# One core, attention plus a gated feed-forward block: engines in written order, row-tiled score tails, row-major sums, Silu on ACT, K transposed by DMA and O by one DMA per step

## The chip, the cores and the metric

The kernel runs on one core of a Trainium2 chip. The metric is the device time of that core in microseconds (us); each kernel was run several times and the median is quoted. The engines are called as the profile calls them: PE (matrix engine), PEld (its weight loads), DVE (vector engine), ACT (scalar engine), POOL (GpSimd), SP (the engine that issues most DMAs).

## The reference, cut to what matters

```python
xn = layernorm(x)                                  # x: 2048 x 640, bf16
q  = (xn @ wq)                                     # 32 heads of 192
k, v = last 512 of the 2048 rows of each head's cache
p  = softmax(q @ k.T * 192**-0.5)                  # no mask
s  = concat_heads(p @ v) @ wo                      # wo: 6144 x 640
g  = silu((silu(xn @ w_gate) * (xn @ w_up)) @ w_down)   # F = 1536
return x + s * g
```

The kernels take two heads at a time ("a pair"; 16 pairs) and 512 rows of x at a time ("a block"; 4 blocks). They subtract the mean over the keys from K, which a softmax does not notice. A head has 192 = 128 + 64 columns: a "main" part that fills the 128 rows of the PE array, and a "tail" of 64.

## The kernel before

Its instructions are placed by a scheduler. Four parts matter. First, K is transposed by PE, main parts as 128x128 tiles and tails as column tiles of the array (128x64). Second, the tails of the two heads of a pair share one 128-row tile of Q, and the K tail of a head is padded with zeros in the other head's rows, so that a tail costs as much as a main:

```python
for kc in range(KC):                       # K transposes
    nc.tensor.transpose(kt[:, 0, kc*P:(kc+1)*P], K_cur[:, hh, kc, 0:DM], ident[:])
for kc in range(KC):
    nc.tensor.transpose(kt[tb:tb+DT, 1, kc*P:(kc+1)*P], K_cur[:, hh, kc, DM:Dh], ident[:])
nc.vector.memset(khat[ob_rows, 1, :], 0.0)
...
for kc in range(KC):                       # scores: one tile of 512 columns, two buffers
    sc = aps.tile([P, 512], dt.float32, name="sc", tag="sc", bufs=2)
    nc.tensor.matmul(sc[:], khat[:, 0, kc*P:(kc+1)*P], qT_m[:, cols], start=True, stop=False)
    nc.tensor.matmul(sc[:], khat[:, 1, kc*P:(kc+1)*P], qT_tail[:, cols], start=False, stop=True)
    p_t = ppool.tile([P, 512], dt.bfloat16, name="p_t")
    nc.scalar.activation(p_t[:], sc[:], ACT.Exp, scale=att_scale)
```

Third, the output projection is computed transposed (512 rows of x as columns) and summed over the pairs in `saccT`, so that the end needs transposes of fp32 tiles. Fourth, O is transposed by 240 small DMAs.

```python
for j in range(3):                         # output projection, transposed
    nc.tensor.matmul(sT_ps[:, :], wo_t[:, j, c*P:(c+1)*P], OT_t[:, j, b*512:(b+1)*512], ...)
nc.vector.tensor_tensor(saccT[:, c, cols], saccT[:, c, cols], sT_ps[:, :], ALU.add)
...
for c in range(c0 // P, c1 // P):          # final tile: fp32 transposes back
    nc.tensor.transpose(so_ps[:, cc*P:(cc+1)*P], saccT[:, c, t*P:(t+1)*P], identf[:])
nc.vector.tensor_tensor(prod[:, c0:c1], so_ps[:, 0:c1-c0], g2_t[:, c0:c1], ALU.mult)
...
nc.gpsimd.tensor_tensor(ob[:], prod[:], x_t[:], ALU.add)
```

The softmax here doesn't subtract the row's maximum and nothing guards it: scores larger than these inputs give would overflow.

## Time and profile before

The median is 1082.95 us (1082.24 to 1084.11). Split into three stretches, of which the last begins with the start of the last exp, the kernel spends:

| stretch | before, us | PE busy in it |
|---|---|---|
| launch to first score matmul (layernorm, feed-forward) | 205.7 | 182.5 |
| first score matmul to start of the last exp (attention) | 848.0 | 842.1 |
| start of the last exp to the end (drain) | 29.4 | 16.4 |

The table is read from the windows view of before; each line has the window, its length, then the busy time of PE, PEld, DVE, ACT and POOL (with the number of instructions), the granted PE clock (1.00 is full), the share of the DMA engines and GB/s:

```profile
0.00:205.70 205.70, 182.45 (x1020) 90.09 (x1020) 103.26 (x195) 61.51 (x98) 27.72 (x47) 0.99 0.24 83
205.70:1053.70 848.00, 842.13 (x5195) 468.08 (x5196) 551.62 (x1830) 400.79 (x709) 107.95 (x150) 1.00 0.25 60
1053.70:1083.10 29.40, 16.36 (x109) 9.86 (x106) 16.70 (x41) 2.35 (x4) 20.14 (x24) 0.86 0.43 139
```

PE is the bound. The page of before says so in the busy line (busy us, share of the span, instructions) and in the chain of waits:

```profile
PE 1040.9 (96%) x6320; PEld 568.0 (52%) x6320; DVE 671.6 (62%) x2065; ACT 464.7 (43%) x811; POOL 155.8 (14%) x219
PE 91%; DMA 2%; DVE 2%; POOL 1%; ACT 1%; issue 1%; POOLq 0%; SPq 0%; ACTq 0%; DVEq 0%
```

Busy is not the same as streaming. The trace's matmul durations are modelled: 379 ns for a 512-column matmul although the next one starts 215 to 216 ns later. What counts is the distance between starts: 216 ns for 512 columns, 83 for 193, 56 for 128, in both kernels, and 136 for 320, which only the changed one has. Summing these (and 109 for an fp32 transpose) over all matmuls gives 992 us of streaming before. The groups that the change touches are these (line, engine, operation, out<-in, shapes, count; then busy us and mean ns; then idle time before it and its releaser):

```profile
L392 ACT ACTIVATE p_t<-sc 128x512 bf16<-128x512 f32 x512 | 286.3, 595 | 318.7 <-PE sc L387 318.5
L263 PE MATMUL sT_ps<-OT_p,wo_p 128*128 128x512 bf16 x960 | 257.4, 379 | 1.1 <-DVE saccT L274 0.6
L274 DVE TENSOR_TENSOR saccT<-saccT,sT_ps 128x512 f32<-128x512 f32 x300 | 202.0, 680 | 44.0 <-PE sT_ps L263 41.0
L404 PE MATMUL pv<-V_h,p_t 128*128 128x193 bf16 x2048 | 213.7, 246 | 0.0
L387 PE MATMUL sc<-qT_tail,khat 128*128 128x512 bf16 x512 | 191.0, 379 | 1.2 <-DVE khat L375 1.2
L362 PE MATMUL kt<-ident,K_p 128*128 128x128 bf16 x128 | 14.8, 219 | 0.1
L364 PE MATMUL kt<-ident,K_p 128*64 128x128 bf16 x128 | 13.1, 225 | 0.0
```

L387 is the zero-padded tail: 512 matmuls of 216 ns, 110 us of streaming, half of it zeros. L362 and L364 are the K transposes.

The timeline of before shows small losses that neither busy time nor the waits view records (start us, us, engine, line, operation, out<-in, count):

```profile
311.28 0.41 PE L404 MATMUL pv<-V_h,p_t 128*128 128x193 bf16 x3
311.70 0.38 PE L383 MATMUL sc<-qT_m_2929,khat 128*128 128x512 bf16 x1
311.91 0.38 PE L387 MATMUL sc<-qT_tail,khat 128*128 128x512 bf16 x1
312.18 0.38 PE L383 MATMUL sc<-qT_m_2929,khat 128*128 128x512 bf16 x1
```

Three PV matmuls need 0.25 us, but the score matmul after them starts 0.42 us later. From 311.91 to 312.18 it is 0.27 instead of 0.216: the next score tile is still being read by an exp. The modelled durations (0.41, 0.38) cover these gaps, so the view of waits shows next to nothing.

The timeline also shows what a change of the array's tiling costs:

```profile
302.03 0.39 PE L362 MATMUL kt<-ident,K_p 128*128 128x128 bf16 x4
302.34 0.41 PE L364 MATMUL kt<-ident,K_p 128*64 128x128 bf16 x4
302.69 0.82 PE L263 MATMUL sT_ps<-OT_p,wo_p 128*128 128x512 bf16 x3
```

Four 56 ns transposes take 0.22 us, but the column-tiled ones start 0.31 us after the first: the last hand-over is 149 ns, 93 more than 56. On the way out it is 151 to 152.

### The profile page before, as it was taken

To read this page: it belongs to the slowest core of one execution; us is meant where nothing else is said; L and a number is where in the kernel's file an instruction comes from. 1 tells how busy PE (TensorE), PEld (TensorE's weight loads), DVE (VectorE), ACT (ScalarE), POOL (GpSimd) and SP (SyncE) were. 2 spreads that over 40 slices of the span, in tenths; PEclk is the share of its full clock that TensorE was granted. 3 is DMA by queue.
4 is the path that set the end of the run, shared out by engine and by line. 5 is a ranking of instruction groups with operands and counts; after the bars stand their busy time and mean duration, and the time that the engine had idled before them with its cause. 6 is when DMAs were issued, how large, how long until landed. Compare 5 with 4: busy or idle time off the path is not lost.

```text
span 1083.1 us, 17198 instructions
## 1 busy us (share of the span) xinstructions
PE 1040.9 (96%) x6320; PEld 568.0 (52%) x6320; DVE 671.6 (62%) x2065; ACT 464.7 (43%) x811; POOL 155.8 (14%) x219
## 2 busy tenths in 40 slices
PE   2999999899999999999999999999999999999985
PEld 1454444465555555555555555555555555555553
DVE  6644544263566757575758484848484848575775
ACT  2422222456545454535354545354544444444520
POOL 4400000200111111111111111111102010000066
PEclk9999999999999999999999999999999999999998
DMA  9400000212323131313131313131313140302034
GB/s 353 123 25 13 13 25 19 88 44 50 88 52 78 48 81 45 81 44 83 43 85 42 86 44 84 42 81 44 87 39 93 33 84 22 86 8 59 1 108 136
DMA packets 118724, 72.05 MB, mean 67 GB/s; under 512 B 103536, under 2 KB 110192, under 8 KB 118640
## 3 DMA queue, kind: packets, MB, share of 16 engines
q0 software_dynamic: 12080, 39.47, 12.5%
q1 hardware_dynamic: 106560, 31.49, 12.2%
q8 instruction: 50, 0.82, 0.3%
q14 instruction: 34, 0.28, 0.1%
HBM read 42.07 MB, written 5.24 MB: 44 GB/s over the span
## 4 chain that ended last, share of the span: by engine, by line
PE 91%; DMA 2%; DVE 2%; POOL 1%; ACT 1%; issue 1%; POOLq 0%; SPq 0%; ACTq 0%; DVEq 0%
PE sT_ps L263 19%; PE pv L404 15%; PE sc L383 12%; PE sc L387 10%; PE qkA L332 6%; PE qkB L339 6%; PE qkC L346 6%; PE gu L200 5%; PE gu L205 5%; PE dn L222 2%; DMA x_blk<-in_A_x_dram 2%; ACT p_t L392 1%; PE kt L364 1%; POOL ob L300 1%; PE kt L362 1%
## 5 line engine op out<-in xcount | busy, mean ns | idle before, releaser
L392 ACT ACTIVATE p_t<-sc 128x512 bf16<-128x512 f32 x512 | 286.3, 595 | 318.7 <-PE sc L387 318.5
L263 PE MATMUL sT_ps<-OT_p,wo_p 128*128 128x512 bf16 x960 | 257.4, 379 | 1.1 <-DVE saccT L274 0.6
L274 DVE TENSOR_TENSOR saccT<-saccT,sT_ps 128x512 f32<-128x512 f32 x300 | 202.0, 680 | 44.0 <-PE sT_ps L263 41.0
L404 PE MATMUL pv<-V_h,p_t 128*128 128x193 bf16 x2048 | 213.7, 246 | 0.0
L404 PEld LDWEIGHTS <-p_t 128*128 128x128 bf16 x2048 | 176.7, 97 | 60.7 <-DVE O_p L421 13.5
L387 PE MATMUL sc<-qT_tail,khat 128*128 128x512 bf16 x512 | 191.0, 379 | 1.2 <-DVE khat L375 1.2
L372 DVE TENSOR_REDUCE ssum<-kt 128x1 f32<-128x512 bf16 x64 | 43.7, 684 | 160.4 <-PE kt L364 160.1
L263 PEld LDWEIGHTS <-wo_p 128*128 128x128 bf16 x960 | 89.8, 97 | 92.7 <-issue 2.5
L412 DVE RECIPROCAL r<-pv 128x1 f32<-128x1 f32 x512 | 74.4, 159 | 75.5 <-PE pv L404 75.5
L414 DVE TENSOR_SCALAR O_p<-pv,r 128x192 bf16<-128x192 f32 x256 | 102.3, 414 | 7.0 <-DVE r L412 3.7
L124 POOL DMA_DIRECT2D V_h<-in_A_v_cache_dram x32 | 24.7, 772 | 461.7 <-PE sc L387 266.6
L421 DVE TENSOR_SCALAR O_p<-pv,r 128x128 bf16<-128x128 f32 x256 | 87.6, 342 | 0.0
L332 PE MATMUL qkA<-xnT,wq_p 128*128 128x512 bf16 x320 | 85.5, 383 | 1.6 <-DVE g_t L229 1.6
L387 PEld LDWEIGHTS <-khat 128*128 128x128 bf16 x512 | 49.3, 97 | 68.3 <-issue 39.2
L339 PE MATMUL qkB<-xnT,wq_p 128*128 128x512 bf16 x320 | 84.6, 380 | 0.0
L346 PE MATMUL qkC<-xnT,wq_p 128*128 128x512 bf16 x320 | 80.1, 379 | 0.0
L418 DVE TENSOR_SCALAR O_p<-pv,r 128x64 bf16<-128x64 f32 x256 | 72.1, 282 | 5.2
L383 PEld LDWEIGHTS <-khat 128*128 128x128 bf16 x512 | 49.3, 97 | 46.1 <-DVE khat L375 4.5
L200 PE MATMUL gu<-xnT,wg_sb 128*128 128x512 bf16 x240 | 60.2, 380 | 0.8 <-DVE hT L213 0.8
L210 ACT ACTIVATE sig<-gu 128x512 bf16<-128x512 f32 x48 | 28.7, 597 | 75.2 <-PE gu L205 75.2
L205 PE MATMUL gu<-xnT,wu_sb 128*128 128x512 bf16 x240 | 60.3, 382 | 0.0
L343 ACT CAST qT_tail<-qkB 128x512 bf16<-128x512 f32 x63 | 36.9, 585 | 50.7 <-PE qkB L339 50.7
(168 smaller groups left out, 931.0 us busy)
## 6 DMA issues: line engine op xcount, KB each, us to landing
K_p<-in_A_k_cache_dram POOLq DMA_DIRECT2D x16, 384.0 KB, 3.5
V_h<-in_A_v_cache_dram POOLq DMA_DIRECT2D x32, 192.0 KB, 3.2
wo_p<-in_A_wo_dram POOLq DMA_DIRECT2D x32, 160.0 KB, 2.6
wq_p<-in_A_wq_dram POOLq DMA_DIRECT2D x16, 240.0 KB, 3.8
OT_p<-O_p SPq DMA_TRANSPOSE x240, 2.3
x_blk<-in_A_x_dram SPq DMA_DIRECT2D x4, 640.0 KB, 9.5
wq_p<-in_A_wq_dram POOLq DMA_DIRECT2D x16, 160.0 KB, 3.2
wo_p<-in_A_wo_dram POOLq DMA_DIRECT2D x32, 80.0 KB, 2.5
```

The costliest lines, as they stand in the source:

```text
L200: nc.tensor.matmul(gu[:, 0, :], wg_sb[:, c, f * P : (f + 1) * P], xnT[:, c, qcols], start=(c == 0), stop=(c == NC - 1),)
L205: nc.tensor.matmul(gu[:, 1, :], wu_sb[:, c, f * P : (f + 1) * P], xnT[:, c, qcols], start=(c == 0), stop=(c == NC - 1),)
L263: nc.tensor.matmul(sT_ps[:, :], wo_t[:, j, c * P : (c + 1) * P], OT_t[:, j, b * 512 : (b + 1) * 512], start=(j == 0), stop=(j == 2),)
L274: nc.vector.tensor_tensor(saccT[:, c, b * 512 : (b + 1) * 512], saccT[:, c, b * 512 : (b + 1) * 512], sT_ps[:, :], ALU.add,)
L332: nc.tensor.matmul(qkA[:, :], wq_cur[:, c, 0:DM], xnT[:, c, cols], start=(c == 0), stop=(c == NC - 1),)
L339: nc.tensor.matmul(qkB[:, :], wq_cur[:, c, DM : DM + 2 * DT], xnT[:, c, cols], start=(c == 0), stop=(c == NC - 1),)
L346: nc.tensor.matmul(qkC[:, :], wq_cur[:, c, Dh + DT : 2 * Dh], xnT[:, c, cols], start=(c == 0), stop=(c == NC - 1),)
L383: nc.tensor.matmul(sc[:], khat[:, 0, kc * P : (kc + 1) * P], qT_m[:, b * 512 : (b + 1) * 512], start=True, stop=False,)
L387: nc.tensor.matmul(sc[:], khat[:, 1, kc * P : (kc + 1) * P], qT_tail[:, b * 512 : (b + 1) * 512], start=False, stop=True,)
L392: nc.scalar.activation(p_t[:], sc[:], ACT.Exp, scale=att_scale)
L404: nc.tensor.matmul(pv[:, s, 0 : Dh + 1], Ps[kc][:, qt * P : (qt + 1) * P], V_h[:, kc, 0 : Dh + 1], start=(kc == 0), stop=(kc == KC - 1),)
L414: nc.vector.tensor_scalar(O_p[:, t, 0:Dh], pv[:, s, 0:Dh], r[:], None, op0=ALU.mult)
```

## The change

It is a rewrite with one intent: keep PE streaming, and stream fewer columns. Every engine is given its instructions in the order in which they are written. A step is one block of one pair (64 steps), and PE's stream in a step mixes work of four steps: scores of step i, PV of step i-1, output projection of step i-3, Q of step i+1. The core of the diff, cuts marked by "...":

```diff
+    ctx.enter_context(tc.manual_schedule())
...
-                    nc.tensor.transpose(kt[:, 0, kc * P : (kc + 1) * P], K_cur[:, hh, kc, 0:DM], ident[:])
+        nc.sync.dma_start_transpose(
+            out=d["KT"][:, 0:3, j * P : (j + 1) * P],
+            in_=d["K"][:, j, :, :].rearrange("p h d -> p (h d)"),
+        )
...
+    def scores(i, kcs):                       # two key chunks, two heads: two tiles of 2 x 512
+        scs = [(kc, sc_tile()) for kc in kcs]
+        for kc, sc in scs:
+            for h in range(2):
+                nc.tensor.matmul(sc[:, h, :], khat[:, 2 * h, ks], qT[:, 2 * h, :], start=True, stop=False)
+        for kc, sc in scs:
+            for h in range(2):
+                r = slice(h * 64, (h + 1) * 64)       # tails: 64 rows, no padding
+                nc.tensor.matmul(sc[:, h, :], khat[r, 1, ks], qT[r, 1, :], start=False, stop=True)
+        for kc, sc in scs:
+            nc.scalar.activation(p_t[:, :, :], sc[:, :, :], ACT.Exp, scale=scale)
...
+    def wo_half(i, qt, n):                    # output projection, row-major, 320 columns
+        ps = mm_tile()                        # mm: two buffers, shared with Q
+        for j in range(3):
+            nc.tensor.matmul(ps[:, 0:HD], OTs[i][:, 3 * qt + j, :], pairs[pr]["wo"][:, j, cols], ...)
+        ...
+            nc.vector.tensor_tensor(sacc[:, t, cols], sacc[:, t, cols], ps[:, 0:HD], ALU.add)
+            if pr == NPAIR - 2 and n == 1:
+                pre_final(t)                  # GpSimd: load x, sacc = sacc * g + x
+        else:                                 # last pair
+            if i >= NS - 2 and n == 0:
+                nc.scalar.copy(s_f[:], ps[:, 0:HD])
+                nc.gpsimd.tensor_tensor(s_f[:], s_f[:], g2[:, t, cols], ALU.mult)
+                nc.gpsimd.tensor_tensor(obs[t][:, cols], s_f[:], sacc[:, t, cols], ALU.add)
+            else:
+                nc.vector.tensor_tensor(s_f[:], ps[:, 0:HD], g2[:, t, cols], ALU.mult)
+                nc.vector.tensor_tensor(obs[t][:, cols], s_f[:], sacc[:, t, cols], ALU.add)
...
+            order = ("A", 0, 1, "q0", 2, 3, "B", 4, "q1", 5, 6, "q2", 7)
+        for step in order:      # "A", "B": two key chunks of scores; "q0".."q2": Q;
+            ...                 # a number: a "unit", one wo_half and then one PV of 4 matmuls
```

Also: Silu comes from ACT's own function instead of Sigmoid and a multiply; g stays on chip; a step's O is transposed by one DMA (63 in all) instead of four; 16 warm-up matmuls and small x loads precede the weights.

## The prediction

> **What bounds the kernel now.** TensorE. The busy table gives PE 1040.9 of 1083.1 us, DVE 671.6, ACT 464.7; the chain of waits is 91% PE. The PE clock is near full speed throughout. Successive matmul starts in the timeline: 216 ns for 512 columns, 83 to 86 ns for 193 (PV), about 56 ns for 128. So streamed columns bound PE, with three losses: (a) the start: x is first used at 23.7 us, gate matmuls run steadily only from 34.7; (b) PV-to-score hand-overs that take about 250 ns instead of 85, and score-to-score ones of 273 instead of 216, because two one-bank score tiles wait for a 595 ns exp: about 25 us; (c) the hand-over to attention (204 to 211 us) and the final stage (1026 to 1083 us, PE 41 of 57 us), about 20 us together.
>
> **What the change removes, adds, moves (PE).**
> - K transposes (256) go to DMA: their line sums give -23 us, with their mode switches.
> - fp32 output transposes go (sums are row-major): -14 us.
> - Score tails: 512 zero-padded 512-column matmuls become 512 matmuls of 64 rows, in pairs on different row halves. The Trainium skill (TensorE: Matmul & The Clock Gate, Part 3) says such matmuls run concurrently; no run shows it yet. If so -55 us (256 x 216 ns).
> - Against that, the skill (TensorEngine Tiling, Key Properties) says a change of tiling mode drains the array. The trace agrees for column tiles: 128x128 to 128x64 and back costs 149 to 152 ns instead of 56, so 95 ns a switch. 256 switches: +24 us.
> - Output projection: 960 x 216 becomes 1536 x about 136 (estimate, 320 columns): neutral.
>
> **Other engines, per step of 64** (estimates from the traced durations): ACT 4 exps of 1024 columns at about 1.02 us plus 3 casts of 0.585 = 5.8 us; DVE 8 sums at 0.48, 4 normalisations at 0.55, reciprocals, K: about 7.4 us. PE: 15x216 + 8x216 + 4x216 + 32x85 + 24x136 = 11.8 us, plus 0.38 us of switches. PE stays the bound; score tiles now own four banks with filler between, so loss (b) should mostly vanish. The two projection buffers may wait on DVE/ACT: I allow 0.2 us a step.
>
> **Sum.** First gate matmul at 11 us (small x pieces ahead of weights); FFN 163 us of streaming plus 4; attention 64 x 12.4 = 793 us; drain after PE's work about 8 us (GpSimd arithmetic, store). Total about **980 us** (0.905 of before); 8 in 10: 952 to 1022. Faster by over 2%: 0.95; within: 0.03; slower: 0.02.
>
> **What would show each step.** Groups: tail matmuls L355 starting in pairs within a few ns, four tails in about 0.43 to 0.6 us. Timeline: a step repeats every 12.2 to 12.5 us. Waits: PE waits for exp nearly nil; waits of L412 for DVE and L158 for ACT under 0.3 us a step. First gate matmul near 11 us. DMA table: O transposes (4x larger) land in well under a 12 us step; no L412 weight load waits for them. DVE 55 to 60% busy, ACT about 40%.
>
> **What would make it wrong.** Tails serial: +55 us (about 1035). Switches dearer for row halves than the 95 ns measured for column halves: each 100 ns is 26 us. Projection buffers stalling PE: each 0.5 us a step is 32 us. O transposes by DMA slower than a step: one stall per step.

## The result, and the profile after

The changed kernel takes 1005.28 us (1004.59 to 1007.32), against 1082.97 us for the one before in the same rounds. The ratio is 0.9282, with a 95% interval of 0.9268 to 0.9295. A ratio here is always the mean time of one kernel's runs over the mean of the other's runs of the same rounds, so it is not quite the ratio of the medians. The prediction was 980 with a range of 952 to 1022: the time lies in the range, 25 us above the centre. All outputs are right.

Here are the busy line of the page after, the groups that answer to those above, and the three stretches in the windows view of after:

```profile
PE 974.6 (97%) x6540; PEld 564.7 (56%) x6540; DVE 522.7 (52%) x1265; ACT 421.1 (42%) x561; POOL 151.5 (15%) x188
L419 DVE TENSOR_TENSOR sacc<-sacc,mm 128x320 f32<-128x320 f32 x448 | 217.6, 486 | 294.4 <-PE mm L412 291.7
L360 ACT ACTIVATE p_t<-sc 128x1024 bf16<-128x1024 f32 x256 | 248.1, 1020 | 229.9 <-PE sc L355 229.8
L412 PE MATMUL mm<-wo_p,OT_b 128*128 128x320 bf16 x1536 | 293.9, 301 | 11.5 <-DVE s_f L431 11.1
L355 PE MATMUL sc<-qT,khat 64*128 64x512 bf16 x512 | 77.5, 381 | 0.0
```

```profile
0.00:183.20 183.20, 173.85 (x976) 93.52 (x977) 58.18 (x120) 56.26 (x101) 24.51 (x48) 0.97 0.33 83
183.20:963.20 780.00, 778.53 (x5427) 456.65 (x5426) 435.21 (x1089) 358.97 (x448) 102.47 (x115) 1.00 0.34 71
963.20:1003.20 40.00, 22.21 (x142) 14.53 (x139) 29.26 (x57) 5.92 (x14) 24.54 (x26) 0.82 0.27 84
```

The first stretch shrank by 22.5 us and attention by 68.0. The drain grew from 29.4 to 40.0 us. Streaming sums to 917 us (992 before; a pair of tails counts once), 75 less, and the span fell by 80. In the first stretch the feed-forward and the layernorm stream 160.4 us in both kernels, so what it gained is work of attention that moved out of it (7 us by the same count) and waiting; no run separates the small x pieces, Silu, the warm-up matmuls and the new order there.

**The tails.** In the timeline of after, a score group looks like this:

```profile
501.04 1.02 PE L347 MATMUL sc<-qT,khat 128*128 128x512 bf16 x4
501.99 0.60 PE L355 MATMUL sc<-qT,khat 64*128 64x512 bf16 x4
502.53 0.58 PE L412 MATMUL mm<-wo_p,OT_b 128*128 128x320 bf16 x3
```

Four mains need 4 x 216 = 863 ns, but the tails start 0.95 us later: 95 ns for entering the 64-row mode. The four tails then last 0.54 us. By the starts of single instructions, the two tails of a pair begin 2 to 4 ns apart, the next pair 222 ns later, and the matmul after them 308 ns after that, 92 more than 216. The first projection after it is another 10 ns slow. So 2 x 216 instead of 4 x 216 is real, and a pair of switches, with the small offsets between the tails, costs about 210 of the saved 432 ns.

**The step.** A step repeats every 12.42 us; every fourth, with the K sums, takes 12.57; the mean is 12.46. Summing starts, 11.76 us of this is streaming and 0.42 switches. The rest are two hand-overs, of which the timeline shows the second:

```profile
503.28 1.24 PE L158 MATMUL mm<-xnT,wq_p 128*128 128x512 bf16 x5
504.36 0.57 PE L412 MATMUL mm<-wo_p,OT_b 128*128 128x320 bf16 x3
504.56 0.59 ACT L163 CAST qT<-mm 128x512 bf16<-128x512 f32 x1
504.77 0.50 PE L373 MATMUL pv<-V_b_210,p_t 128*128 128x193 bf16 x4
505.20 0.57 PE L412 MATMUL mm<-wo_p,OT_b 128*128 128x320 bf16 x3
```

The Q chunk (L158) and the projections (L412) take turns on two buffers `mm`. The chunk's buffer is read by the cast, which ends at 505.15; the second projection needs that buffer and starts at 505.20. Between lie one projection (0.41 us) and one PV (0.33), which end 97 ns too early. At the first chunk of a step the same gap is 152 ns, and in one step of four a K sum on DVE holds a buffer for 154 ns. None of it is in the view of waits, because the modelled PV time of 0.50 covers it.

**The start.** The first gate matmul starts at 12.0 us. Then the timeline shows a stall:

```profile
23.21 0.89 DVE L207 BATCH_NORM_STATS2 stats<-x_t 128x6 f32<-128x320 bf16 x2 [5.82 <-DMA x_t<-in_A_x_dram]
24.26 0.64 DVE L257 TENSOR_TENSOR hT<-sc,sg 128x512 bf16<-128x512 f32 x1
24.95 1.44 PE L251 MATMUL sc<-xnT,wg_sb 128*128 128x512 bf16 x3 [4.60 <-DVE hT L257]
```

DVE has the layernorm statistics of x tile 4 written ahead of a multiply that frees a score tile. The load of tile 4 was issued after the loads of the feed-forward's weights (5.9 MB, all but a twelfth of it on the same queue), so the multiply, which could run at 21, waits with it, and PE waits for the multiply. The clock records show PE at half clock from 22.5 to 29.3 us.

**The drain.** The view of waits of after has two large entries for PE (waited for: us in total, times, longest):

```profile
PE mm L412 <- DVE s_f L431: 11.1, 15, 1.7
PE sc L251 <- DVE hT L257: 4.6, 1, 4.6
```

The second is the start. The first is the last pair. Its windows (same columns as above), and five lines of its timeline:

```profile
956.00:976.50 20.50, 15.36 (x99) 9.79 (x98) 18.41 (x31) 4.21 (x5) 15.87 (x14) 0.79 0.39 100
984.00:1003.20 19.20, 7.89 (x54) 4.88 (x53) 9.44 (x19) 4.60 (x12) 14.26 (x16) 0.88 0.22 78
```

```profile
967.71 0.48 DVE L431 TENSOR_TENSOR s_f<-mm,g_76 128x320 f32<-128x320 f32 x1
967.98 1.41 POOL L403 TENSOR_TENSOR sacc<-sacc,g_76 128x640 f32<-128x640 f32 x1
968.23 1.52 DVE L432 TENSOR_TENSOR ob<-s_f,sacc 128x320 bf16<-128x320 f32 x1
974.90 0.95 DVE L432 TENSOR_TENSOR ob<-s_f,sacc 128x320 bf16<-128x320 f32 x1
976.29 0.49 DVE L432 TENSOR_TENSOR ob<-s_f,sacc 128x320 bf16<-128x320 f32 x1
```

In the last pair each half of a projection needs two DVE operations (but for the first halves of the last two blocks, which ACT and GpSimd close). The second, L432, has both sources on chip in SBUF and takes 0.49 us alone (976.29), but 1.52 us beside GpSimd's `sacc * g` (968.23). All nine such operations that start while one of GpSimd's closing multiplies or adds runs (957 to 976 us) end 0.35 to 0.36 us after that GpSimd operation ends: here 967.98 + 1.41 = 969.39, and 968.23 + 1.52 = 969.75. The GpSimd operation keeps its 1.40 us. L431, which reads PSUM, stays at 0.48. This agrees with the Trainium skill (SBUF — State Buffer, "SBUF: two separate sides"), which says that the port pair shared by the two engines is an exclusive lock, held for a whole instruction, for which a DVE operation with two SBUF inputs competes.

GpSimd is still at this work because each of its tiles (1.40 + 1.40 us) waits another 0.6 to 0.9 us for its own load of x and spends 0.58 on issuing it. In the last two blocks GpSimd itself is the bound, with 0.79 and 0.98 us per tile in turn. The clock records show half clock from 968.0 to 978.2 us, though the longest PE gap before it was 1.73 us. The half clock does not set the length of this stretch: in e4, with the same code there, it lasts 6.8 us instead of 10.2, and the drain is 39.9 us instead of 40.0.

### The profile page after: what moved, and what is told of

The parts are those of the page before. It is cut to its first block, busy times and chain, and to the rows that moved or that the text cites. A ratio compares the mean times of both kernels' runs of the same rounds, so it can differ in the third digit from the quotient of the medians.

```text
span 1003.2 us, 16007 instructions
## 1 busy us (share of the span) xinstructions
PE 974.6 (97%) x6540; PEld 564.7 (56%) x6540; DVE 522.7 (52%) x1265; ACT 421.1 (42%) x561; POOL 151.5 (15%) x188
## 5 line engine op out<-in xcount | busy, mean ns | idle before, releaser
L419 DVE TENSOR_TENSOR sacc<-sacc,mm 128x320 f32<-128x320 f32 x448 | 217.6, 486 | 294.4 <-PE mm L412 291.7
L360 ACT ACTIVATE p_t<-sc 128x1024 bf16<-128x1024 f32 x256 | 248.1, 1020 | 229.9 <-PE sc L355 229.8
L412 PE MATMUL mm<-wo_p,OT_b 128*128 128x320 bf16 x1536 | 293.9, 301 | 11.5 <-DVE s_f L431 11.1
L158 PE MATMUL mm<-xnT,wq_p 128*128 128x512 bf16 x960 | 238.2, 379 | 0.0
L412 PEld LDWEIGHTS <-OT_b 128*128 128x128 bf16 x1536 | 139.0, 97 | 144.9 <-issue 69.8
L163 ACT CAST qT<-mm 128x512 bf16<-128x512 f32 x192 | 112.3, 585 | 192.9 <-PE mm L158 184.4
L382 DVE TENSOR_TENSOR O_b<-pv,r 128x384 bf16<-128x384 f32 x256 | 142.7, 557 | 8.8
L347 PE MATMUL sc<-qT,khat 128*128 128x512 bf16 x512 | 131.8, 379 | 1.1 <-ACT qT L163 0.9
L158 PEld LDWEIGHTS <-wq_p 128*128 128x128 bf16 x960 | 90.7, 97 | 69.3 <-issue 0.8
L373 PE MATMUL pv<-V_b_210,p_t 128*128 128x193 bf16 x768 | 96.2, 249 | 0.0
L373 PE MATMUL pv<-V_b_214,p_t 128*128 128x193 bf16 x640 | 79.5, 246 | 0.0
L373 PE MATMUL pv<-V_b_212,p_t 128*128 128x193 bf16 x640 | 79.5, 246 | 0.0
L347 PEld LDWEIGHTS <-khat 128*128 128x128 bf16 x512 | 48.1, 97 | 32.4 <-issue 2.0
```

What stands on the lines that cost most here:

```text
L158: nc.tensor.matmul(q_ps[:, :], pairs[pr]["wq"][:, c, j * P : (j + 1) * P], xnT[:, c, b * 512 : (b + 1) * 512], start=(c == 0), stop=(c == ...
L163: nc.scalar.copy(qTs[i][:, j, :], q_ps[:, :])
L347: nc.tensor.matmul(sc[:, h, :], khat[:, 2 * h, ks], qT[:, 2 * h, :], start=True, stop=False)
L360: nc.scalar.activation(p_t[:, :, :], sc[:, :, :], ACT.Exp, scale=scale)
L373: nc.tensor.matmul(acc[:, h, 0 : Dh + 1], Ps[i][kc][:, h, qt * P : (qt + 1) * P], V_p[:, kc, h, 0 : Dh + 1], start=(kc == 0), stop=(kc == ...
L382: nc.vector.tensor_tensor(Obs[i][:, qt, :, :], acc[:, :, 0:Dh], r[:].to_broadcast([P, 2, Dh]), ALU.mult)
```

## The experiments

Ratios to before are compared. One hundredth of a ratio is 10.8 us. The expectations count the last stretch from the last first-half group of score matmuls to the end (46.9 us in after); in the text below the drain is counted from the start of the last exp (40.0 us in after).

| run | median us | ratio to before | 95% interval | typical step, us | drain, us |
|---|---|---|---|---|---|
| the change | 1005.28 | 0.9282 | 0.9268 to 0.9295 | 12.42 | 40.0 |
| e3_order | 998.91 | 0.9203 | 0.9184 to 0.9222 | 12.28 | 39.9 |
| e1_padded_tails | 1025.83 | 0.9457 | 0.9443 to 0.9472 | 12.71 | 38.4 |
| e2_switch_twice | 1025.30 | 0.9450 | 0.9435 to 0.9464 | 12.70 | 39.1 |
| e4_x_ahead | 998.54 | 0.9199 | 0.9183 to 0.9215 | 12.42 | 39.9 |
| e5_k_on_pe | 1023.08 | 0.9435 | 0.9421 to 0.9449 | 12.42 | 40.1 |
| e6_xr_ahead | 1012.51 | 0.9323 | 0.9299 to 0.9347 | 12.42 | 33.2 |
| e7_drain_split | 1002.99 | 0.9247 | 0.9227 to 0.9267 | 12.42 | 25.5 |
| e8_all | 989.45 | 0.9123 | 0.9110 to 0.9137 | 12.33 | 25.7 |
| e9_pv_first | 1004.75 | 0.9256 | 0.9243 to 0.9270 | 12.44 | 40.0 |
| e10_xr_quiet | 1004.13 | 0.9274 | 0.9233 to 0.9315 | 12.42 | 33.2 |
| e11_all_mended | 982.38 | 0.9050 | 0.9033 to 0.9066 | 12.44 | 25.0 |
| e12_final | 973.19 | 0.8952 | 0.8918 to 0.8987 | 12.18 | 23.8 |

My theory was that the 25 us above the centre lie in the drain (two DVE operations per half, slowed by GpSimd's late arithmetic), with small parts at the start and in the step's buffer hand-overs. The rivals were that the tails save less than computed, or that the array's mode switches cost more.

### e3_order: other places for the Q chunks

```diff
-            order = ("A", 0, 1, "q0", 2, 3, "B", 4, "q1", 5, 6, "q2", 7)
+            order = ("A", 0, 1, 2, "q0", 3, "B", 4, 5, "q1", 6, "q2", 7)
```

> Only the places of two Q-projection chunks in a step's written order change (first chunk after projection unit 2 instead of 1, second after 5 instead of 4). Theory A (the 0.25 us idle per step in front of two output-projection groups is a wait for a two-buffer PSUM tile that a Q chunk holds while its cast queues behind two 1.02 us exps): the two waits of about 152 and 97 ns vanish, a step falls from 12.42 to about 12.17 us, the time to about 990 us (-15). Rival B (the gap comes from the PE switching between operand kinds, or from the DVE sums): the gap only moves, time stays within 3 us of 1005.

The step fell to 12.28 us, as the wait of 152 ns at the first chunk went; the 97 ns stayed and moved before the third chunk, and the step with the K sums has a wait of 247 ns. Only half of what was expected came (12.17 us a step, 990 us). The mean step is 12.35 instead of 12.46, about 7 us over 64 steps. The ratios give 8.5 us (0.0079), the profiled spans 5.2, as the stall at the start was longer in this profile (7.7 us instead of 4.6; its length differs from run to run). So this hand-over is a matter of the written order. e1 and e2 are built on this kernel.

### e1_padded_tails: the zero-padded tails put back

```diff
-                    sc[:, h, :], khat[r, 1, ks], qT[r, 1, :], start=False, stop=True
+                    sc[:, h, :], pad[:, h, ks], qT[:, 1, :], start=False, stop=True
```

`pad` has one tile per head with zeros in the other head's rows; they are written once, and the centring of K writes the other half.

> The reordered kernel with the row-half tails undone: 512 zero-padded 128-row tails. Theory A (pairs truly run together and two switches per group cost about 95 and 105 ns): a group of four mains and four tails takes 8 x 216 = 1726 ns instead of about 1495, +0.23 us twice a step, about +29 us against the reordered kernel. Rival B (the switches eat the pairing): within 5 us of the reordered kernel.

Against e3 the ratio rises by 0.0254, 27.5 us (give or take about 2.6 by the two intervals); the step goes from 12.28 to 12.71 us, and 0.43 x 64 is also 27.5. So the row-tiled tails give 27.5 us net of their switches, where the prediction had 55 - 24 = 31. The rival that the tails fail to pay falls.

### e2_switch_twice: eight changes of mode in a step instead of four

```diff
         for kc, sc in scs:
             for h in range(2): ...mains...
-
-        for kc, sc in scs:
             for h in range(2): ...tails...
```

> The reordered kernel with main and tail matmuls alternating per 128 keys instead of per 256, so 8 mode switches a step instead of 4. Theory A: each switch costs about 95 to 100 ns of TensorE, +0.39 us a step, about +25 us against the reordered kernel. Rival B (the cost beside a tail group is not per switch but the fill of the first tail, hidden otherwise): under +8 us.

Against e3 the ratio rises by 0.0247. By the medians that is 26.4 us for 256 more switches (12.28 to 12.70 us a step), 103 ns each, near the 95 that the prediction took from column tiles. Doing the tails of two key chunks together, as the change does, is therefore worth as much as the tails' whole net gain. The Trainium skill (TensorEngine Tiling (Array Packing), Key Properties) says that a change of tiling mode drains the array, which agrees; it gives no size.

### e4_x_ahead: x tiles 4 to 7 loaded before most of the weights

```diff
-        lnx = fctx.enter_context(tc.tile_pool(name="lnx", bufs=6))
+        lnx = fctx.enter_context(tc.tile_pool(name="lnx", bufs=8))
         for q in range(4):
+            if q == 1:
+                for t in range(4, 8):
+                    load_x(t)
...
-                if nx and f == 0:
+                if nx and b > 0 and f == 0:
```

> The changed kernel with the x tiles of the second query block issued before the later weight quarters rather than after all weights. Theory A (4.6 us of the start are lost since DVE, in written order, waits for x tile 4 before it may multiply hidden block 1): that wait goes, FFN ends about 4 to 5 us earlier, time about 1000.5. Rival B (the weights themselves come too late): gate matmuls then wait for a weight quarter instead, time within 1.5 us of 1005.

The stall of 4.6 us is gone, and with it the second half-clock window of the start. The first score matmul starts at 176.3 us instead of 183.2, and the ratio is 0.0083 lower (9.0 us; the profiled spans differ by 7.1). The span's gain is more than the stall; that the rest, some 2.5 us, came from the clock fits a window of 6.8 us at half clock, but was not separated.

### e5_k_on_pe: K transposed by PE again

```diff
-        nc.sync.dma_start_transpose(out=d["KT"][:, 0:3, ...], in_=d["K"][:, j, :, :]...)
+        ktp = psum.tile([P, 3, P], bf, name="ktp", tag="mm", bufs=2)
+        for c in range(3):
+            nc.tensor.transpose(ktp[:, c, :], k_f[:, c * P : (c + 1) * P], ident[:])
+        nc.vector.tensor_copy(out=d["KT"][:, 0:3, ...], in_=ktp[:, :, :])
```

The three transposes per key chunk go through an `mm` buffer, all as 128x128 tiles.

> The changed kernel with only the K transposes put back on TensorE: 12 per head pair, through a PSUM tile and a DVE copy; O stays on DMA. Theory A (each transpose costs its 56 ns stream on the bound engine, and its PSUM tile takes turns with the projection's): 192 x 56 ns = 10.8 us plus up to 0.3 us of buffer wait per group of three, so +11 to +30 us, 1016 to 1035. Rival B (off the critical path either way; the DMA move bought nothing): within 4 us of 1005.

The ratio rises by 0.0153, 16.6 us. In the steady part all of it lies in one step of four, which takes 13.66 instead of 12.42 us: four times three transposes, whose groups take 408, 407, 256 and 167 ns up to the next matmul, instead of 168. So only 0.67 us of the 1.24 is transposing; the other 0.57 (8.5 us over 15 pairs) comes behind the transposes, where the next matmul needs an `mm` buffer, and this placement may be to blame for it. Against transposes on PE done in this way, moving K to DMA is worth about 17 us, of which some 10 is streaming; the prediction had 23 from the line sums of before, which hold the column tiles' switches.

### e6_xr_ahead: x for the closing arithmetic loaded ahead

```diff
     def pre_final(t):
-        x_r = finp.tile([P, D], bf, name="x_r")
-        nc.gpsimd.dma_start(out=x_r[:], in_=x2[t * P : (t + 1) * P, :])
+        if t in (4, 8):
+            load_xr(t // 4 + 1)               # a tile of 4 x 128 rows, two buffers
...
             load_pair(pr)
+            if pr == NPAIR - 4:
+                load_xr(0)
+                load_xr(1)
```

> The changed kernel with the x rows of the closing residual loaded long ahead, four tiles at a time, so GpSimd no longer waits 0.65 us and issues a DMA between its two 1.4 us ops per tile. GpSimd's pre-final work should then end near 958 us instead of 975. Theory A (the DVE adds with two SBUF sources take 0.97 us instead of 0.49 while GpSimd computes, and DVE bounds the last pair): the adds after 958 us fall to 0.49 us, the stretch from the last score group to the end shrinks from 46.9 to about 40 us, time about 999. Rival B (the stretch is bound by PE's half clock or by the stores): it stays within 2 us.

The drain shrank as the theory says, from 40.0 to 33.2 us, and yet the kernel is not faster: 0.9323 against 0.9282. The view of waits of e6 has a new first entry, and the tile view of OT_b has a new maximum (after: 3.6/3.8/9.7):

```profile
PE mm L420 <- DMA OT_b<-O_b: 13.6, 1, 13.6
DMA to landing us min/median/max: 3.6/3.9/26.4
```

One transpose of O took 26.4 us, two steps. At that time the two x loads (2 x 640 KB) were in flight with K (384 KB), wq (480) and wo (480) of the next pair, in all some 2.6 MB; the x loads themselves took up to 22.9 us. The projection comes three steps after its scores and has less than two steps of slack. So the expected 999 us was missed by the experiment's own making, and the expected gain went into a new wait. That these loads delayed the transpose is read from the timing; e10 and e11 test it in part.

### e7_drain_split: the last pair's closing shared out, on top of e6

```diff
-            if i >= NS - 2 and n == 0: ...ACT copies, GpSimd multiplies and adds...
-            else: ...DVE multiplies and adds...
+            nc.vector.tensor_tensor(s_f[:, cols], ps[:, 0:HD], g2[:, t, cols], ALU.mult)
             if n == 1:
+                nc.gpsimd.tensor_tensor(obs[t][:], s_f[:], sacc[:, t, :], ALU.add)
```

DVE does one operation per half, from PSUM, and GpSimd the addition with two SBUF sources, once per tile.

> As the run with x loaded ahead, and in the last pair DVE only multiplies out of PSUM (0.48 us a half) while GpSimd does all closing adds (1.4 us a tile). Theory A (DVE's op count bounds the drain): last stretch about 28 to 32 us instead of 46.9, time 987 to 991. Rival B (GpSimd then bounds it, its adds slower than 1.4 us beside DVE): last stretch 38 us or more, time 996 or more.

The drain is 25.5 us, 7.7 less than in e6 and 14.5 less than after. In the count of the expectation it is 32.4 us, about the top of the expected 28 to 32. The kernel keeps e6's stall (10.3 us here), so its time misses the expected 987 to 991 and hardly differs from after: 0.9247. The drain is thus confirmed as the large term, but not yet banked.

### e8_all: e4, e7 and an order with later Q chunks

```diff
+            order = ("A", 0, 1, 2, "q0", 3, "q1", "B", 4, 5, 6, "q2", 7)
```

The K sums move to units 0, 2 and 4.

> All mendings together: x tiles ahead of the later weights (-6.9 us as measured), the drain split, a third order (first Q chunk after unit 2, second right after unit 3 and before the second score group, third after unit 6) and K sums moved to even units. If the leftover waits are only exp-queued casts and DVE sums, a step falls from 12.42 to about 12.17 us in all four kinds (-16 us). Sum about 963 to 970 us. If DVE or ACT have hidden limits at this pace: over 975.

0.9123, 989.45 us, a miss: 963 to 970 had been expected. The parts add up: the start gave its 7 us, the drain its 14, the step 0.09 us (not the expected 0.25; a wait of 148 ns ahead of the third chunk stayed), and a stall of 8.8 us on a transpose of O took its share back.

### e9_pv_first: PV ahead of the projection in each unit

```diff
-                if O: wo_half(i - LAG, step // 2, step % 2)
                 if V: pv(i - 1, step // 2, step % 2)
+                if O: wo_half(i - LAG, step // 2, step % 2)
```

The K sums and centring move to units 1, 4 and 6. The idea was that a cast then has PV, projection, PV in front of the next use of its buffer.

> The changed kernel with PV before the projection in each unit, K sums after units 1, 4, 6; the order of Q chunks untouched. A cast lands about 0.89 us after its last matmul starts to be followed, and the second projection after a Q chunk started 0.74 us after it; PV first makes that 1.08 us. Theory A (all steady idle time is this two-buffer wait): 152 and 97 ns and the 154 ns of K sums vanish, a step falls from 12.42 to about 12.15 us, time about 988. Rival (ACT or DVE have no more room): the wait moves elsewhere, 998 or more.

This missed: 12.44 us a step where 12.15 had been expected. The waits behind the first two chunks and the one for the K sums are gone, but one of 262 ns appeared ahead of the third chunk. The timeline of e9 shows it:

```profile
516.14 0.56 DVE L382 TENSOR_TENSOR O_b<-pv,r 128x384 bf16<-128x384 f32 x1
516.61 0.96 DVE L419 TENSOR_TENSOR sacc<-sacc,mm 128x320 f32<-128x320 f32 x2
517.14 1.24 PE L158 MATMUL mm<-xnT,wq_p 128*128 128x512 bf16 x5
```

The third chunk (L158) takes the `mm` buffer of the projection two before it. That buffer is freed by the first of the two sums (L419), which in written order stands behind the normalisation of PV (L382). The first sum ends about 517.1, and the chunk starts at 517.14. With PV first, a sum queues behind a reciprocal and a normalisation whenever the unit ends a PV tile.

### e10_xr_quiet: e6 with the x loads elsewhere

```diff
+        elif k == 2 and u == 2 and pr in (NPAIR - 4, NPAIR - 3):
+            load_xr(pr - NPAIR + 4)
```

One x tile is loaded in each of two pairs, two blocks after the pair's own loads.

> The earlier run with the x rows loaded ahead, but the two 640 KB loads issued in the middle of a step without a pair load, one in each of two pairs. Theory A (the 13.6 us stall of that run came from my loads beside the pair's loads slowing an O transpose, and had nothing to do with the drain): no stall, last stretch stays at about 40.6 us instead of 46.9, time about 999. Rival (the loads disturb wherever they stand): a stall of some us again, over 1003.

The drain is e6's 33.2 us. The longest landing of a transpose fell from 26.4 to 16.2 us and the longest stall from 13.6 to 3.3. The time is 0.9274, with one run of 1011.93 among 1004: over the 1003 us set for the rival. So this run does not show that quiet loads cost nothing; the place is still not quiet. POOL issues in order, and the load of wo waits for its buffer, so that the x load comes out right beside the next pair's loads (e12's timeline shows the same: 23.28 us idle before the issue of wo, then x, then K):

```profile
738.93 0.77 POOL L119 DMA_DIRECT2D wo_p<-in_A_wo_dram  x1 [23.28 <-PE mm L423]
739.70 0.80 POOL L343 DMA_DIRECT2D x_r<-in_A_x_dram  x1
740.47 1.49 POOL L104 DMA_DIRECT2D K_p<-in_A_k_cache_dram  x2
```

In e10 the DVE additions of the last pair (L440 here), up to 984 us, no longer meet GpSimd's arithmetic, except the first, and alone they take 0.49 us:

```profile
964.57 1.19 DVE L440 TENSOR_TENSOR ob<-s_f,sacc 128x320 bf16<-128x320 f32 x1
966.20 0.49 DVE L440 TENSOR_TENSOR ob<-s_f,sacc 128x320 bf16<-128x320 f32 x1
```

This is the second half of the proof that the overlap, and not the operation, was slow.

### e11_all_mended: e4, e7, e9 and the placement of e10

```diff
+                eng = nc.vector if i == NS - 1 and qt % 2 else nc.gpsimd
+                eng.tensor_tensor(obs[t][:], s_f[:], sacc[:, t, :], ALU.add)
```

DVE also takes the additions of every second tile of the last block.

> All together: x ahead of the later weights (-6.9), PV first (-16), quiet x loads, DVE multiplies and GpSimd adds in the last pair with two of the last four adds on DVE (last stretch about 30 us instead of 46.9, -17). Sum about 963 to 970 us, 0.89 to 0.895 of before. Over 975 would mean that the parts collide.

0.9050, 982.38 us, with no stall on a transpose; it missed the expected 963 to 970, which counted 16 us for PV first, and e9 shows that this gains no time in the step. The loads of e10 did no harm here (the longest step is 12.45 us, the longest landing 9.4). Against after that is 0.0232 or 25 us, a little more than the 7 us (start) and 15 us (drain) that the spans of e4 and e7 show separately.

### e12_final: PV first in even units, projection first in odd ones

```diff
-            order = ("A", 0, 1, "q0", 2, 3, "B", 4, "q1", 5, 6, "q2", 7)
+            order = ("A", 0, "q0", 1, 2, "q1", 3, 4, "B", 5, 6, "q2", 7)
...
+                if V and step % 2 == 0: pv(i - 1, step // 2, 0)
                 if O: wo_half(i - LAG, step // 2, step % 2)
+                if V and step % 2: pv(i - 1, step // 2, 1)
```

In this order a PV tile is filled by two PVs in a row, a chunk's next buffer use is far enough behind, and no sum stands behind a normalisation that PE waits for. K sums and centring follow units 2, 4 and 6.

> As the run with all mended, with the order chosen so that no projection or Q chunk asks for its PSUM tile sooner than the cast (about 0.85 us after the chunk) or the sum (behind reciprocal and normalisation) can give it back: PV first in even units, projection first in odd ones, Q chunks after units 0, 2 and 6, second score group after unit 4, K sums after units 2, 4, 6. Theory A (all steady idle time was order, none of it capacity): a step falls to about 12.15 us, time about 963 to 968. Rival (something has no room left at that pace, or the O transposes come late): 975 or more.

0.8952, 973.19 us (967.37 to 974.12): the best kernel, 3.6% below the change by the ratios, though above the expected 963 to 968. By the starts of its matmuls, a typical step of 12.18 us is 11.76 of streaming and 0.42 of mode switches, and nothing else. The step is as expected; in the waits of the profiled run stalls on transposes of O remain, one of them of 3.9 us:

```profile
PE mm L423 <- DMA OT_b<-O_b: 4.5, 3, 3.9
```

One run of the four took 967.37 us; whether it had no such stall is open, as there is no trace of it.

## Why the prediction was right or wrong, point by point

The prediction of faster was right, and the mechanism of each large step was right. The sum came out 24 us below the profiled span of 1003.2 us (the times quoted are about 2 us above the spans), and the terms can be set side by side. The measured column is read from the trace, counting the three Q chunks that run before the first score (3.2 us) as attention and the 15.7 us of PE streaming that remain when the last exp starts as attention too:

| term of the sum | predicted, us | measured, us |
|---|---|---|
| first gate matmul | 11 | 12.0 |
| feed-forward | 163 + 4 | 168.0 |
| attention, 64 steps | 64 x 12.4 = 793 | 798.9 |
| drain beyond PE's work | 8 | 24.3 |
| sum | about 980 | 1003.2 (span) |

- **The term that was mis-sized is "drain after PE's work about 8 us (GpSimd arithmetic, store)".** It measured 24.3 us, 16 of the 24 missed. I had costed the end as one GpSimd operation and one store after a PE that streams to its end. Taken literally that was right: from PE's last matmul (start 996.28, modelled 0.30 us) to the end it is 6.6 us. The other 17.7 us lie before it, while PE still has work: 10.7 of them are in the view of waits, cut to this window, as PE waiting for L431 to free an `mm` buffer. What the runs showed in its place: most projection halves of the last pair need two DVE operations (0.48 + 0.49 us, and 0.36 of normalisation beside them, against 0.74 us of PE work in a unit), one of them waits out whole GpSimd operations of 1.40 us, GpSimd is late because it loads its x itself, and in the last blocks GpSimd is the bound. Loading x ahead took 6.8 us off (e6, e10), sharing the operations out another 7.7 (e7).
- **Attention, +5.9 us.** The mean step is 12.46, in the predicted band of 12.2 to 12.5, and 0.06 x 64 = 3.8 us. The remaining 2 us lie at the ends of the pipeline and I have not resolved them. The allowance of 0.2 us a step for the two projection buffers was about right (0.25 in three steps of four, 0.40 in the fourth), and e12 shows that another order does without these waits.
- **Tails.** Pairs start 2 to 4 ns apart, as the Trainium skill (TensorE: Matmul & The Clock Gate, Part 3) draws it (about 4 ns). Net gain 27.5 us (e1) against 31 predicted. A switch of row halves, the late first projection after it included, costs 103 ns (e2) and not 95, which is 2 us of the difference; the rest is within the intervals.
- **K transposes.** 17 us (e5, half of it waits for a buffer that e5 shares) against 23. The line sums used in the prediction are of modelled durations and hold switches of the column tiles.
- **The fp32 transposes at the end** (14 us of line sums before) are gone from the profile after. No run put them back alone.
- **Loss (b).** In the trace after, the 165 score-to-score hand-overs (6.6 us) and the 132 slow PV-to-score ones (15.6 us) are gone; PE never waits for an exp. No run undid this part alone, so its share (22 us, where the prediction had about 25) is read from the trace only.
- **O transposes by DMA** land in 3.8 us in the median and 9.7 at most, below a step of 12 us. This was right for after, and e6 showed how thin it is: 26.4 us beside some 2.6 MB of other loads.
- **Start.** 12.0 against 11. The prediction misread the trace of before here: x is not first used at 23.7 us but at 5.1, and the first gate matmul runs at 18.6 (steady matmuls from 34.7, as it says). The allowance of 4 us for the feed-forward is nearly what was lost (5.0), but by luck: nearly all of it is one stall that the prediction did not know of and that e4 took away.
- **Busy shares.** ACT 42% (about 40 predicted); DVE 52% (55 to 60 predicted, a little too high).

The prediction's list of what would make it wrong named the tails, the switches, the buffers and the transposes of O. It did not name the drain, a term that had no duration from the trace beside it.

## What to carry to other kernels

Cost the last stretch like a loop of its own, engine by engine: here, once PE streamed nearly all the time, the end was bound by the engines that do the closing arithmetic, and operations with two SBUF sources on DVE took up to 1.53 us instead of 0.49 while GpSimd computed. With engines in written order, a wait on one late load or one queued sum holds everything written after it, so place each producer of a buffer by the units of PE work that hide it, and measure gaps by the distance between starts, as modelled durations hide gaps below some 165 ns (379 - 215 in these traces). Before moving loads "ahead", look at what else is in flight and at which transfer PE will wait for next.

## What the Trainium skill lacked or had wrong

- TensorEngine Tiling (Array Packing), Key Properties: it says that a mode change drains the array, but gives no size. Here a change between 128-row and 64-row mode costs 95 ns on the way in, 92 on the way out and about 10 on the next matmul, or 103 ns per switch by e2; column halves cost 93 to 96.
- TensorE: Matmul & The Clock Gate, "Back-to-back issue gap": it gives about 131 ns for a sustained stream of weight load and 512-column matmul, and 81 ns for 128 columns. Both traces here have 215 to 216 ns and 55 to 56 ns, with a weight load for every matmul; the page's other figures (216 and 56, which this section gives to an isolated matmul) are the ones that held.
- TensorE: Matmul & The Clock Gate, Part 1: its table has half clock after an idle window of about 3.4 us, and a later section tells of a case with frequent short idles, without a number for them. Here the clock was halved from 968.0 to 978.2 us though the longest PE gap ahead of it was 1.73 us and PE was busy for 15.36 of 20.5 us (956.0 to 976.5).
- SBUF — State Buffer, "SBUF: two separate sides": the exclusive lock is stated and is confirmed (DVE operations of 0.49 us stretched up to 1.53 us). It gives no lag for such a pair of arithmetic operations: the DVE operation ended 0.35 to 0.36 us after the GpSimd one in all nine cases of 957 to 976 us.
- DMA: Bandwidth & Descriptors, "Rules for kernel authors": it says that a transpose next to ordinary DMAs needs nothing, in a row on corrupted results. That held for the results; for the time it is not enough: 3.8 us in the median against 26.4 us beside some 2.6 MB of loads (e6). No page gives a size for this.
